# Threshold attention and Fourier mixing on one core: the last group's two closing products without the inner level, u's forms spread between products, the last fold placed by hand

## The chip, the cores and the metric

The kernel runs on one core of one Trainium2 chip. The time is the device time of one execution in microseconds (us), the median of several runs. Lower is better. Line numbers (L1306) are those of the kernel before the change, unless it is said otherwise.

## The reference, cut to what matters

```python
scores = scale * q @ k.T                       # 8 batches x 8 heads, 576 x 576, 64 deep
attn = softmax of the scores within tau of each row's maximum, 0 elsewhere
x = attn @ v, heads side by side               # (8, 576, 512)
u = x + real(fft(fft(x, axis=1), axis=2))
un = (u - mean(u)) / sqrt(var(u) + 1e-6)       # over the 512 channels
out = u + relu(un @ w_ch1) @ w_ch2             # w_ch1 512 x 2048, w_ch2 2048 x 512
```

All is computed in fp32.

## The kernel before, in words

**The two halves.** The attention half goes through 8 batches, 4 pairs of heads each, 5 tiles of queries a pair: 160 steps. A batch's weighted values are folded by symmetry (`fold_rows`, DVE L678 to L694 for the last pair of a batch; `fold_chunks` L709 and L710; further folds in `mixing`, L731 to L740) and turned by small matrix products into u, kept transposed in `u_t` (py L750, pa L767 and L771, u_t L792 and L796).

The channel half takes the 4608 rows of u in 9 groups of 512. Group 0 is computed plainly (`channels`). Groups 1 to 8 go through `two_level`. The first stage multiplies by w1: 4 parts with 7 products each (a Strassen scheme in Winograd's form, in the order 1, 2, 5, 6, 4, 7, 3), PE L1163. The second multiplies by w2 with two levels of the same scheme: 7 outer products (`L1` = 1, 2, 5, 4, 6, 7, 3), each made of 7 inner ones (`J`) of 4 matmuls, PE L1306, 28 matmuls to an outer product. Normalisation is applied at the end, where a product is added to u with the factor `rstd` (`Rows.add`, DVE L863); `Rows.store` (L870) writes 128 finished rows from SP's queue.

**The forms.** A Strassen scheme multiplies sums and differences of its blocks. On the side of u there are four per group: t1, t2, -t4, t3 (`u_form`, L1087; two instructions each, on DVE for groups 7 and 8, on POOL before). The inner forms of the left operand of the second stage are s1 and s2 on DVE and s3 and s4 on POOL (`l2_forms`, L1144), made during the outer product before; the outer ones are `l1_form` (L1121: a21, s1 and a12, a quarter at a time). The forms of the weights are made once, during groups 0 and 1, by `w1_forms` and `w2_forms` (L977), and written to DRAM as blocks of 128x512: 28 in f1 and 49 in f2, seven per outer product. A form of w2 is stored by `keep`: two inner blocks (L987), the last (L991), and the four computed ones (L998) out of a room in `w1[3]` which the next form's blocks are written into.

**What sets the order.** The code is written in the order in which each engine shall work; there is no scheduler behind it. `fill` lets as much of the channel half go ahead as the budget of a slot allows; in the steps of the attention half three calls of it stand between parts of the softmax. The weight blocks come in loads of four (`ensure`, L1036) into a ring of three buffers, two loads ahead. Small jobs of DVE and POOL in the second stage are placed by hand at slots (outer product, inner product) with `at_slots`. All PSUM tiles of the products come out of four banks.

**The first stage's evictions.** In a part, product 1 is copied from its bank by ACT (L1172), product 2 is added by DVE (L1100) and put through relu by ACT (L1105), product 5 is copied by ACT (L1174). Product 6 accumulates in product 1's bank and DVE adds it to product 5's copy (L1100). Product 4 is copied by ACT (L1182). Product 7 accumulates in that same first bank and is added to two results at once (L1100, 128x1024); product 3 follows in a bank of its own. In the code all four u forms are issued ahead of the first product.

**The second stage's results.** v_u, v_11, v_22, v_21 and v_12 hold outer results in seven inner pieces each (896 columns). ACT copies (L1321) or DVE adds (L1323, L1326) each outer product into them. `gather` sums the seven inner pieces of a result in five additions (L1213), and `finish` adds them to u (L863). For groups 1 to 7 the gathers are on POOL, in the next group's time. For the last group there is no next one: they are on DVE, in slots of the last product (3), whose bank is evicted in pieces.

**The end of the attention half.** The loop over steps runs three steps beyond the last (L1635), in which the last tile's weights, the last product with v (`values_in_parts`, pv L627, copied by ACT L634), the last fold and the last `mixing` come.

Of the kernel before, what the change touches and what calls it, by code (L numbers as in the profile page):

```python
# [9 lines left out]
FP32 = mybir.dt.float32  # L10
# [37 lines left out]
def kernel(  # L48
# [874 lines left out]
    J = (1, 2, 5, 4, 6, 7, 3)  # L923
    HH = HID // 2
    f1 = dram.tile([128, 28, 512], FP32, name="f1")
    f2 = dram.tile([128, 49, 512], FP32, name="f2")

    def w1_forms():

# [37 lines left out]
    def w2_forms():  # L967
# [11 lines left out]
        def keep(m, at):  # L979
            x = b[at]  # L980
            i = 7 * L1.index(m)
            to = f2[:, i : i + 7, :].rearrange("p j (s n) -> p j s n", n=128)
            quarter = {
                (k, n): x[:, 4 * k : 4 * k + 4, 128 * n : 128 * n + 128]
                for k in range(2) for n in range(2)
            }
            nc.sync.dma_start(  # L987
                out=f2[:, i : i + 2, :].rearrange("p j (s n) -> p (j s) n", n=128),
                in_=x[:, :, 0:128],
            )  # L990
            nc.sync.dma_start(out=to[:, 6], in_=quarter[1, 1])  # L991
            t1, minus_t4, t2, t3 = (room[:, j] for j in range(4))
            combine(nc.vector, t1, quarter[0, 1], quarter[0, 0])
            combine(nc.gpsimd, t3, quarter[1, 1], quarter[0, 1])
            yield
            combine(nc.vector, t2, quarter[1, 1], t1)
            combine(nc.gpsimd, minus_t4, quarter[1, 0], t2)
            nc.sync.dma_start(out=to[:, 2:6], in_=room)  # L998
            yield
# [25 lines left out]

    PER = 4
    LOADS = [(f1, 28, k) for k in range(0, 28, PER)] + [(f2, 49, k) for k in range(0, 49, PER)]
    issued = 0

    def ensure(n):  # L1030

        nonlocal issued
        while issued <= n and issued < (NG - 1) * len(LOADS):
            src, count, k = LOADS[issued % len(LOADS)]
            n_blocks = min(PER, count - k)
            nc.sync.dma_start(  # L1036
                out=w1[issued % 3][:, 0 : 512 * n_blocks].rearrange("p (j n) -> p j n", n=512),
                in_=src[:, k : k + n_blocks, :],
            )
            issued += 1  # L1040

    def block(g, second, index):

# [18 lines left out]
    def two_level(g, rows):  # L1062
# [25 lines left out]
                    out=out_[:, c], in0=in0[:, c], in1=in1[:, c], op=ALU.subtract  # L1088
                )

        u_form(t1, b[0, 1], b[0, 0])
        u_form(t2, b[1, 1], t1)
        u_form(minus_t4, b[1, 0], t2)
        u_form(t3, b[1, 1], b[0, 1])
        right = {
            1: b[0, 0], 2: b[1, 0], 3: b[1, 1], 4: minus_t4, 5: t1, 6: t2, 7: t3,
        }
# [50 lines left out]
        for part in range(4):  # L1148
# [4 lines left out]
            for at, m in enumerate(ORDER):  # L1153
# [30 lines left out]
                elif m == 7:  # L1184
                    twice = bass.AP(
                        tensor=bank.tensor, offset=bank.offset,
                        ap=[list(bank.ap[0]), [0, 2], [1, 512]],
                    )
                    add(both, twice)
                    relu(both)  # L1190
                else:
                    add(h01, bank[:, :])
                    relu(h01)
                next(forms, None)
                tick()
                if part == 3 and g > 1 and at in (2, 3, 5):
# [23 lines left out]
        def gather(eng, v):  # L1220
# [7 lines left out]
                plus(eng, v[:, 2:4], twice(v[:, 5])),  # L1228
            ]

        def finish(i, n, v):
            if wanted:
                wanted.pop().factors()
# [20 lines left out]
            for jn, job in zip(slots, jobs, strict=True):  # L1254
                side.setdefault((at, jn), []).append(job)

        for at in range(6):
            def next_form(at=at):
                if at not in coming:
                    coming[at] = l2_forms(L1[at + 1])  # L1260
# [9 lines left out]
        at_slots(4, (1, 2, 4, 6), l1_form(a12, a12, s1_tile, (P, P, P, P)))  # L1270
        at_slots(2, (0, 1, 2, 3, 4), gather(P, v_11))
        at_slots(4, (2, 4), [lambda n=n: finish(0, 0, v_11)[n]() for n in range(2)])
        at_slots(
            5, (0,), [lambda: P.tensor_tensor(out=v_12, in0=v_u, in1=v_22, op=ALU.add)]
        )
        if g < NG - 1:
            at_slots(6, (0, 1), [plus(P, v_22, v_u), plus(P, v_21, v_u)])
        else:
            at_slots(6, (0, 0), [plus(V, v_22, v_u), plus(P, v_21, v_u)])
            at_slots(6, (1, 1, 1, 1, 1), gather(V, v_22))  # L1280
            at_slots(6, (2, 2), finish(1, 1, v_22))
            at_slots(6, (2, 2, 3, 3, 3), gather(V, v_21))
            at_slots(6, (4, 4), finish(1, 0, v_21))
            at_slots(6, (4,), [stores(2, 3)])
            w = v_12.rearrange("p (j n) -> p j n", n=128)
            at_slots(6, (4,) * 4, [
                plus(V, w[:, 1:5:3], twice(w[:, 0])), plus(V, w[:, 6], w[:, 2]),
                plus(V, w[:, 6], w[:, 4]), lambda: rows.add(0, slice(256, 384), w[:, 1]),
            ])
            second = bass.AP(  # L1290
                tensor=w.tensor, offset=w[:, 3].offset, ap=[list(w.ap[0]), [-128, 2], [1, 128]]
            )
            at_slots(6, (5,) * 4, [
                plus(V, w[:, 5], w[:, 4]), plus(V, w[:, 2:4], twice(w[:, 5])),
                lambda: rows.add(1, slice(256, 512), second), stores(1),
            ])
        for at, m in enumerate(L1):
            for jn, j in enumerate(J):
                cut = g == NG - 1 and m == 3
                if jn in (0, 4) or cut and jn > 4:  # L1300
                    bank = ps.tile([128, 512], FP32, tag="mm", bufs=4, name="po")
                c0 = 0 if cut and jn > 4 else 128 * (jn % 4)
                to = bank[:, c0 : c0 + 128]
                right_ = block(g, True, 7 * at + jn)
                for s in range(4):
                    nc.tensor.matmul(  # L1306
                        to, lefts[m][j][:, s], right_[:, 128 * s : 128 * (s + 1)],
                        start=(jn in (0, 4) or cut and jn > 4) and s == 0, stop=s == 3,
                        skip_group_check=True,
                    )  # L1310
                if jn in (3, 6) or cut and jn > 3:
                    first, end = (0, 512) if jn == 3 else (512, NV)
                    if cut and jn > 3:
                        first, end = 128 * jn, 128 * jn + 128
                    src = bank[:, 0 : end - first]

                    def here(v):
# [3 lines left out]
                        nc.scalar.copy(here({1: v_u, 5: v_22, 4: v_21}[m]), src)  # L1321
                    elif m == 2:
                        V.tensor_tensor(out=here(v_11), in0=here(v_u), in1=src, op=ALU.add)  # L1323
                    else:
                        to = here(v_12 if m == 3 else v_u)
                        V.tensor_tensor(out=to, in0=to, in1=src, op=ALU.add)  # L1326
                while held:
                    held.pop(0)()
                held.extend(side.get((at, jn), ()))
                while held and not holding:  # L1330
                    held.pop(0)()
                if jn == 3 and at < 4:
                    rows.load((2, 3, 0, 1)[at])
                    if at == 3:
# [4 lines left out]
            background()  # L1339
            if m != 3:  # L1340
                yield 2048
        if g == NG - 1:
            w = v_12.rearrange("p (j n) -> p j n", n=128)
            rows.add(0, slice(384, 512), w[:, 6])
            rows.store(0)
            return
        for v in (v_22, v_21, v_12):
            pending.extend(gather(P, v))
# [283 lines left out]

    late.append(True)

    for i in range(2 * per_batch, total + 3):  # L1635


        n, t = divmod(i, NT)
# [52 lines left out]
            load_v(n + 1)  # L1691
        if t == 4 and n + 2 < B * NPAIR:
            load_pair(n + 2)
    ended.append(True)
    per_slot = cost(0) / 40
    while mixes or work:
# [47 lines left out]
```

## Time and profile before

| | |
|---|---|
| median of 3 runs (lowest, highest) | 1607.57 us (1606.21, 1608.24) |
| profiled execution, its own time | 1605.7 us |
| its span | 1603.8 us |
| granted TensorE clock, mean | 0.988 |
| PE busy | 1537.4 us, 96% |
| DVE, ACT, POOL busy | 69%, 57%, 51% |
| chain that ended last | PE 76%, DVE 14%, ACT 4%, issue 2%, POOL 2%, DMA 1% |
| last stage of groups 7 and 8 (first matmul) | 1400.5, 1498.7 us |

The profile is one execution on the chip. A row of the timeline gives the start in us from the span's start, the duration, the engine, the line, the operation, what it writes and reads with the shape, and how many instructions were merged; in brackets stands the idle time of the engine before it and what ended that. PE is the matmul, PEld the weight load beside it. An fp32 matmul of the code stands as two rows in the trace. Ends of matmuls are modelled. SPq is the queue of SP, which issues nearly all transfers.

### The profile page before, as it was taken

How to read it: one execution, taken by the hardware profiler on the slowest of the kernel's cores; microseconds unless marked ns; L12 is line 12 of the kernel's file. 1: busy time of each engine (PE TensorE's matmuls, PEld its weight loads, DVE VectorE, ACT ScalarE, POOL GpSimd, SP SyncE). 2: the span in 40 equal slices, each digit the busy share in tenths (PEclk: the TensorE clock that was granted, in tenths of full speed). 3: DMA queues.
4: the chain of work that ended last, by engine and by line, in shares of the span. 5: the costliest groups of instructions: out<-in, count | busy, mean ns of one | idle time of the engine just before them, and what ended most of it. 6: DMA issues, size and time to landing. Idle time of an engine off the chain costs nothing.

```text
span 1603.8 us, 27061 instructions
## 1 busy us (share of the span) xinstructions
PE 1537.4 (96%) x9770; PEld 1189.2 (74%) x9770; DVE 1105.6 (69%) x2165; ACT 908.4 (57%) x1873; POOL 811.7 (51%) x1014
## 2 busy tenths in 40 slices
PE   8999979999999999999999999999999999999997
PEld 4555445555787778877787878787887778879997
DVE  7997886845869566766577566856676656746547
ACT  5774665554655666656666666656665665223121
POOL 6784664034455552536254724455263625537646
PEclk9999999999999999999999999999999999999998
DMA  6423221555956264634564355626463534546655
GB/s 158 131 57 115 75 76 36 175 158 164 291 159 203 72 182 125 182 104 141 141 175 140 113 159 145 191 69 180 123 185 108 154 113 158 191 157 237 235 193 190
DMA packets 245499, 239.05 MB, mean 149 GB/s; under 512 B 196947, under 2 KB 214869, under 8 KB 225014
## 3 DMA queue, kind: packets, MB, share of 16 engines
q1 hardware_dynamic: 242854, 237.02, 49.1%
q8 instruction: 78, 1.28, 0.3%
q10 hardware_dynamic: 2512, 0.30, 0.2%
q14 instruction: 55, 0.45, 0.1%
HBM read 207.50 MB, written 29.62 MB: 148 GB/s over the span
## 4 chain that ended last, share of the span: by engine, by line
PE 76%; DVE 14%; ACT 4%; issue 2%; POOL 2%; DMA 1%; SPq 0%; DVEq 0%; ACTq 0%; POOLq 0%
PE ph L1163 24%; PE po L1306 17%; PE pv L627 8%; PE sc L427 7%; PE pw L596 6%; PE po L901 4%; PE ph L877 2%; PE py L750 2%; DVE e L467 2%; PE sc L433 1%; PE pa L767 1%; PE pe L578 1%; PE pa L771 1%; DVE neg L451 1%; ACT e L512 1%
## 5 line engine op out<-in xcount | busy, mean ns | idle before, releaser
L512 ACT ACTIVATE e<-sc,neg 128x576 f32<-128x576 f32 x216 | 158.6, 734 | 139.8 <-DVE neg L506 139.4
L506 DVE TENSOR_REDUCE neg<-sc 128x1 f32<-128x576 f32 x216 | 154.0, 749 | 112.0 <-PE sc L427 104.1
L1306 PE MATMUL po<-w,w_all 128*128 128x128 f32 x1792 | 229.1, 278 | 0.7 <-ACT ends L584 0.7
L1306 PEld LDWEIGHTS po<-w,w_all 128*128 128x128 f32 x1792 | 214.7, 193 | 10.2 <-issue 5.5
L1100 DVE TENSOR_TENSOR hs<-ph,hs 128x512 f32<-128x512 f32 (+1 forms) x128 | 105.1, 821 | 158.5 <-PE ph L1163 104.0
L1109 POOL TENSOR_TENSOR w<-hs 128x512 f32<-128x512 f32 x32 | 42.1, 1320 | 318.9 <-ACT hs L1105 245.1
L596 PE MATMUL pw<-ident,e 128*128 128x128 f32 x1152 | 172.1, 276 | 18.0 <-ACT x_first L634 9.1
L1163 PE MATMUL ph<-u_t,w 128*128 128x256 f32 x768 | 180.5, 381 | 0.5 <-DMA w<-f 0.4
L527 DVE SCALAR_TENSOR_TENSOR e<-sc,thr,e 128x576 f32<-128x576 f32 x216 | 168.1, 811 | 17.7 <-ACT thr L516 17.7
L427 PE MATMUL sc<-kT,qT 64*128 64x288 f32 x1024 | 170.3, 432 | 7.9 <-DVE e L467 7.9
L598 ACT COPY e_t<-pw 128x512 f32<-128x512 f32 x256 | 148.5, 594 | 45.8 <-PE pw L596 44.6
L540 ACT ACTIVATE e<-e,den 128x576 f32<-128x576 f32 x216 | 157.6, 775 | 16.6 <-DVE den L534 15.4
L596 PEld LDWEIGHTS pw<-ident,e 128*128 128x128 f32 x1152 | 136.3, 142 | 36.3 <-ACT x_first L634 10.1
L1163 PE MATMUL ph<-w_all,w 128*128 128x256 f32 x672 | 157.0, 382 | 2.9 <-DVE hs L1100 1.8
L1163 PEld LDWEIGHTS ph<-u_t,w 128*128 128x128 f32 x768 | 141.2, 190 | 23.4 <-issue 4.4
L1105 ACT ACTIVATE hs<-hs 128x512 f32<-128x512 f32 (+1 forms) x96 | 74.1, 772 | 122.0 <-DVE hs L1100 120.8
L1163 PEld LDWEIGHTS ph<-w_all,w 128*128 128x128 f32 x672 | 123.5, 190 | 25.6 <-issue 6.2
L427 PEld LDWEIGHTS sc<-kT,qT 64*128 64x128 f32 x1024 | 93.9, 186 | 62.9 <-issue 32.8
L1213 POOL TENSOR_TENSOR w_all<-w_all 128x128 f32<-128x128 f32 (+2 forms) x160 | 118.5, 758 | 29.9 <-DVE w_all L1326 22.4
L1306 PE MATMUL po<-w,hs 128*128 128x128 f32 x960 | 126.3, 279 | 0.0
L1306 PEld LDWEIGHTS po<-w,hs 128*128 128x128 f32 x960 | 116.2, 193 | 9.4 <-issue 7.2
L792 POOL TENSOR_TENSOR u_t<-x,tmp 128x289 f32<-128x289 f32 (+1 forms) x45 | 34.5, 766 | 104.8 <-DVE tmp L787 104.8
(221 smaller groups left out, 2985.1 us busy)
## 6 DMA issues: line engine op xcount, KB each, us to landing
w<-f SPq DMA_DIRECT2D x152, 1024.0 KB, 4.9
hs<-in_moe_w_ch_dram SPq DMA_DIRECT2D x23, 512.0 KB, 4.6
q_in<-in_q_dram SPq DMA_DIRECT2D x128, 72.0 KB, 3.9
out_dram<-u SPq DMA_DIRECT2D x36, 256.0 KB, 2.5
k_in<-in_k_dram SPq DMA_DIRECT2D x124, 72.0 KB, 3.0
v_in<-in_v_dram SPq DMA_DIRECT2D x64, 128.0 KB, 4.7
f<-w SPq DMA_DIRECT2D x14, 512.0 KB, 4.0
f<-w SPq DMA_DIRECT2D x7, 1024.0 KB, 4.4
```

The costliest lines, as they stand in the source:

```text
L427: nc.tensor.matmul(sc[j][:, c, 0:HALF], qT[hp, 128 * t : 128 * t + 128], kT[hp, k0 + HALF * c : k0 + HALF * (c + 1)], start=True, stop=True,)
L506: nc.vector.tensor_reduce(out=neg[:, j : j + 1], in_=sc[j][:, :, 0:HALF], axis=AXIS_XY, op=ALU.max, negate=True,)
L512: nc.scalar.activation(out=ej, in_=sc[j][:, :, 0:HALF], func=ACT.Exp, bias=neg[:, j : j + 1], scale=1.0)
L527: nc.vector.scalar_tensor_tensor(out=ej, in0=sc[j][:, :, 0:HALF], scalar=thr[:, j : j + 1], in1=ej, op0=ALU.is_ge, op1=ALU.mult, accum_out ...
L540: nc.scalar.activation(out=e[:, S * j : S * (j + 1)], in_=e[:, S * j : S * (j + 1)], func=ACT.Copy, scale=den[:, j : j + 1],)
L596: nc.tensor.transpose(pw[:, c, :], e[:, c0 : c0 + 128], ident[:, :])
L598: nc.scalar.copy(e_t[:, 4 * j : 4 * j + 4, qs], pw[:, :, :])
L627: nc.tensor.matmul(pv[64 * j : 64 * j + 64, 0:m], vt[:, 2 * c + j, :], e_t[:, 4 * j + c, 0:m] if c < 4 else ends[:, 0, 0:m], start=(c == 0 ...
L1100: nc.vector.tensor_tensor(out=to, in0=bank, in1=to if other is None else other, op=ALU.add)
L1163: nc.tensor.matmul(bank[:, 256 * q : 256 * q + 256].rearrange("p (two n) -> p two n", two=2), left[:, 256 * c + 128 * q : 256 * c + 128 * ...
L1213: return lambda: eng.tensor_tensor(out=to, in0=to, in1=other, op=ALU.add)
L1306: nc.tensor.matmul(to, lefts[m][j][:, s], right_[:, 128 * s : 128 * (s + 1)], start=(jn in (0, 4) or cut and jn > 4) and s == 0, stop=s == ...
```

## The change

1. **Products 7 and 3 of the last group** have no inner scheme any more. Each is done as 4 blocks of 8 matmuls into two banks (one for each 128 rows), straight from the left operand and the four quarters of w2's outer form. For this `keep` writes seven more blocks of 128x512 to f2 (four at form 3, three at form 7), and the last group's loads end with one of three and one of four blocks. Product 6 is added to v_22 and v_21 at once (DVE), v_u is added to v_22 on POOL and to v_21 on DVE earlier, both results are gathered together (five additions of double width on DVE) while product 7 runs, and go to all four tiles of rows. Products 7 and 3 are added to u directly from PSUM. v_12 isn't formed in this group.
2. **The u forms of groups 7 and 8**: only t1 stands ahead of the first product; t2, -t4 and t3 follow behind the evictions of products 2, 5 and 6 of the first part.
3. **The end of the attention half** is written out in place of the loop's three extra steps. PE's order stays the same. On ACT, the copy of the last pv (L634) moves behind a copy of an outer product and four copies of u. On DVE, `fold_chunks` (L709, L710) comes ahead of one inner form, an eviction and two adds to u, and another inner form comes ahead of two fold instructions.

```diff
-    f2 = dram.tile([128, 49, 512], FP32, name="f2")
+    f2 = dram.tile([128, 56, 512], FP32, name="f2")
...
             nc.sync.dma_start(out=to[:, 6], in_=quarter[1, 1])
+            for n, at_ in {7: ((49, (1, 0)), (50, (1, 1)), (51, (0, 1))),
+                           3: ((52, (0, 0)), (53, (1, 0)), (54, (1, 1)), (55, (0, 1)))}.get(m, ()):
+                nc.sync.dma_start(
+                    out=f2[:, n].rearrange("p (s n) -> p s n", n=128), in_=quarter[at_]
+                )
...
+    ALL_LOADS = LOADS * (NG - 2) + LOADS[:16] + [(f2, 52, 49), (f2, 56, 52)]
...
-        u_form(t1, b[0, 1], b[0, 0])
-        u_form(t2, b[1, 1], t1)
-        u_form(minus_t4, b[1, 0], t2)
-        u_form(t3, b[1, 1], b[0, 1])
+        u_forms = [
+            (t1, b[0, 1], b[0, 0]), (t2, b[1, 1], t1), (minus_t4, b[1, 0], t2),
+            (t3, b[1, 1], b[0, 1]),
+        ]
+        while len(u_forms) > (3 if g >= NG - 2 else 0):
+            u_form(*u_forms.pop(0))
...
+                if at > 0 and u_forms:
+                    u_form(*u_forms.pop(0))
                 next(forms, None)
                 tick()
...
+            at_slots(3, (1,), [plus(P, v_22, v_u)])
+            at_slots(4, (0,), [plus(V, v_21, v_u)])
+            at_slots(5, (0, 0, 1, 1, 2), gather_both())
+            at_slots(5, (2, 3), finish(0, 1, v_22))
+            at_slots(5, (3, 3), finish(1, 1, v_22))
+            at_slots(6, (0, 0), finish(1, 0, v_21))
+            for n in range(2):
+                at_slots(
+                    6, (1,), [lambda n=n: rows.add(2 + n, slice(0, 512), twice(plain[7][n]))]
+                )
+                at_slots(6, (1,), [stores(2 + n)])
...
+        def plain_product(at, m):
+
+            x = a[m].rearrange("p (k s i n) -> p k i s n", k=2, i=2, n=128)
+            banks = plain[m] = [
+                ps.tile([128, 512], FP32, tag="mm", bufs=4, name="po")[:, 0:256] for _ in range(2)
+            ]
+            for jn, (n, k, at_) in enumerate(((0, 0, 0), (0, 1, 1), (1, 1, 2), (1, 0, 3))):
+                right_ = plain_block(m, at_)
+                for i in range(2):
+                    for s in range(4):
+                        nc.tensor.matmul(
+                            banks[i][:, 128 * n : 128 * n + 128], x[:, k, i][:, s],
+                            right_[:, 128 * s : 128 * (s + 1)],
+                            start=jn == 0 and s == 0, stop=jn % 2 == 1 and s == 3,
+                            skip_group_check=True,
+                        )
+                slot(at, jn)
...
+        if whole:
+            while held:
+                held.pop(0)()
+            for n in range(2):
+                rows.add(n, slice(256, 512), plain[3][n])
+                rows.store(n)
             return
...
-    for i in range(2 * per_batch, total + 3):
+    for i in range(2 * per_batch, total):
...
+    values = values_in_parts(B * NPAIR - 1, 1)
+    next(values, None)
+    fill(True)
+    while held:
+        held.pop(0)()
+    next(values, None)
+    while folds:
+        fold_more()
+    last_fold = fold_rows(B * NPAIR - 1)
...
+    start_batch(B - 1)
+    for _ in range(3):
+        mix(1)
+        fill(True)
```

## The prediction

> **What bounds the kernel now.** I read the page first, then the chain of waits from 1380 us on, then the timelines of PE, DVE and SP where the change touches them.
>
> ```profile
> span 1603.8 us, 27061 instructions
> ...
> PE 1537.4 (96%) x9770; PEld 1189.2 (74%) x9770; DVE 1105.6 (69%) x2165; ACT 908.4 (57%) x1873; POOL 811.7 (51%) x1014
> ```
>
> PE is busy 96% of the span, so time is to be had only where PE idles (66 us in all) or after its last matmul. The change touches three such places. The end, from the timeline:
>
> ```profile
> 1588.57 4.71 DVE L1213 TENSOR_TENSOR w_all<-w_all 128x896 f32<-128x896 f32 x6
> ...
> 1589.99 2.84 PE L1306 MATMUL po<-w,w_all 128*128 128x128 f32 x24
> ...
> 1599.32 0.48 DVE L863 SCALAR_TENSOR_TENSOR u<-w_all,rstd,u 128x256 f32<-128x256 f32 x1
> ...
> 1600.04 0.35 DVE L863 SCALAR_TENSOR_TENSOR u<-w_all,rstd,u 128x128 f32<-128x128 f32 x1
> ```
>
> PE's last row ends at 1592.83; DVE works on to 1600.39, and the last store ends the span 3.4 us later. So 7.56 us of gathers and adds lie behind PE. Second, the start of group 7 (start, duration, engine, line; in brackets the idle time before it and what ended it):
>
> ```profile
> 1405.84 1.77 DVE L1087 TENSOR_TENSOR w_all<-u_t,t_room 128x256 f32<-128x256 f32 x2 [1.98 <-POOL u_t L792]
> ...
> 1406.89 4.06 PE L1163 MATMUL ph<-w_all,w 128*128 128x256 f32 x16 [0.96 <-DVE w_all L1087]
> 1407.53 1.27 DVE L1087 TENSOR_TENSOR w_all<-u_t,w_all 128x256 f32<-128x256 f32 x2
> ...
> 1408.72 1.54 DVE L1087 TENSOR_TENSOR w_all<-u_t 128x256 f32<-128x256 f32 x2
> ...
> 1410.18 0.68 DVE L1100 TENSOR_TENSOR hs<-ph,hs 128x512 f32<-128x512 f32 x1
> ...
> 1412.03 0.69 DVE L1100 TENSOR_TENSOR hs<-ph,hs 128x512 f32<-128x512 f32 x1 [1.17 <-ACT hs L1174]
> ...
> 1412.78 1.99 PE L1163 MATMUL ph<-w_all,w 128*128 128x256 f32 x8 [1.83 <-DVE hs L1100]
> ```
>
> All four u forms (L1087) stand on DVE ahead of the first eviction (L1100, 1410.18); ACT's copy of product 5 waits behind that eviction's relu, the second eviction waits for the copy, and product 7, which adds into that bank, waits until 1412.78. Third, the last fold:
>
> ```profile
> 1384.18 0.80 PE L750 MATMUL py<-dim_c,f 128*128 128x128 f32 x2 [2.91 <-DVE f L731]
> 1384.77 1.92 PE L1306 MATMUL po<-w,w_all 128*128 128x128 f32 x8
> ```
>
> PE waits 2.91 us, and the eight rows behind that take 1.92 where eight take 1.06 elsewhere, the next eight 1.91: with the granted clock at 0.91 over 1360 to 1400, the wait costs about 1.7 us more than itself.
>
> **Products 7 and 3 plain: PE.** The old product is 28 matmuls, 56 rows in the trace (each stands twice), and takes 6.25 us (chain of waits, "PE po L1306 x56"), 0.1117 us a row. The plain one is 32 matmuls, 64 rows, 7.15 us; the operand shapes are the same, so I take the same price. Two of them: +1.79 us, all on the path, because PE has no gap from 1498.68 on. PE's end moves from 1592.83 to 1594.62. Their weights are loads of 768 KB and 1 MB, asked for at the first and the fifth block of product 6 (1573.9 and 1577.5); with the 4.9 us of w<-f they land by 1582.4, while the blocks are wanted at about 1582.0 (first, landing 1578.8) and 1587.3: at nothing. The cover is about 3 us; a landing of 9.1 us, the longest in this trace, would cost about 1 us.
>
> **The same: DVE and POOL.** Removed behind PE: the inner forms of products 7 and 3 (L1144), v_12, and the gathers of three results. What is left, in DVE's new order: product 6's second add (768 elements from PSUM; between the rows of 512 at 0.69 and 1024 at 1.22, so 0.96) starts when product 6 ends, 1580.36, and ends at 1581.3. Five joint gathers, two of 512 elements at 0.69 and three of 256 at 0.41 (the quickest L1087), 2.6 us, to 1583.9. Six adds of 128x256 at 0.44 (the pair at 1593.19 took 0.88), to 1586.6. Plain product 7 ends at 1587.5; its two adds of 128x512 take 0.75 each (L863 u<-po), to 1589.0, followed by the stores of rows 2 and 3 on SP, which has no load left behind them. Then DVE is free, 5 us before PE ends. Product 3's first bank is complete eight rows before the end, so its add runs beside PE; the second starts at 1594.65 and takes 0.48 (0.75 for 512 less 0.27 for 256 elements), to 1595.13, against 1600.39 before: **-5.3 us**. The last stores follow close together before and after, 3.4 us.
>
> Here a rule speaks against the change. Rows: DVE's L1144 of 128x512 took 0.69 us at best and 1.58 us in the mean of the four from w that stood beside POOL work. The Trainium skill, page "SBUF — State Buffer", section "Who interferes with whom", says that a DVE instruction with two SBUF inputs is shut out while a GpSimd instruction that reads SBUF holds the shared ports. The new gathers are of this kind, and POOL now does v_22's sum (2.1 us) and all of a12's four parts (1.27 to 1.75 each). Laid out from 1569.5, these and product 6's forms (1.65 and 1.27, the latter not before 1573.3) end at about 1581, as the gathers start. By the free price the sum is 1589.0, as above; by the rule, were POOL busy throughout, two gathers at 1.58, three at 0.94 and six adds at 1.31 make 13.8 us in place of 5.2, and DVE ends product 7's adds at about 1596.6 (0.94 from the slowest L1087, 1.31 from the pair of L863 at 1374.02). I take the free price, since POOL's list is over; the adds from PSUM have one SBUF tensor and stay out of it.
>
> **The u forms.** New order in groups 7 and 8: t1, first eviction, t2, -t4, second eviction, t3. In group 7, t2 still waits for u_t until 1405.84 (POOL, not moved), so the 0.96 us before product 6 stays. The first eviction now runs at 1404.2, in DVE's idle time. Product 6 ends at about 1409.0, product 4 at 1410.7; the second eviction runs 1409.1 to 1409.8, t3's halves come at 1410.5 and 1411.1; product 7 starts at about 1410.7 instead of 1412.78: **-2.1 us**. PE then shows no idle up to group 8, so the gain is kept to the end. In group 8, which has no such wait today, an eviction of 0.69 now stands ahead of t2: with T the end of product 2, t2's halves come at T+1.4 and T+2.1 to 2.3, and PE wants them at T+1.7 and T+2.2: +0.1 (0 to 0.5). Together **-2.0**. Bounds: nothing (each wait returns at t3), and -2.8 (both idle times of group 7).
>
> **The last v product and fold.** PE's order is unchanged there. ACT's copy of x (L634) moves behind five evictions, from 1361.53 to about 1364.8, done at 1365.2; the fold's first step waits for DVE's statistics until 1365.76 anyway. On DVE two fold steps (0.78 and 0.79) move ahead of four other instructions, and one form moves earlier; DVE works without a gap from 1365.76 to 1386, with the same rows ahead of L731, so PE's wait of 2.91 stays. POOL's s4 for product 7 comes about 1.3 us later, to 1376.3, and is wanted at 1378.0. Cost 0; bounds -4.6 (the whole wait and the slow rows behind it) and +0.5 (POOL's overlap falls worse).
>
> **Seven more stores of blocks (f<-w_all, 256 KB).** They stand on SP's queue in the stage of 358 to 417 us: four behind 358.17, three behind 406.83. Queued behind them: v's loads, the row swap at 369.63, the store of the forms' room (L998), and the weight loads. Engine times by stretch (last two numbers: DMA share and GB/s), then SP's timeline:
>
> ```profile
> 400.00:420.00 20.00, 19.23 (x109) 14.95 (x108) 19.52 (x32) 12.06 (x23) 14.11 (x16) 1.00 0.90 291
> ```
>
> ```profile
> 406.83 0.58 SPq L991 DMA_DIRECT2D f<-w_all  x1
> 412.40 0.33 SPq L998 DMA_DIRECT2D f<-w  x1
> ```
>
> Issue is 0.58 each, 1.7 to 2.3 us in a row, and SP stands free for 2.2 and 5.0 us before L998 (v's loads end at 363.61, L991 at 407.41). The DMA engines are 90% busy, so three stores of 0.79 MB at 291 GB/s push the queue out by 2.7 us. L998 then lands at 412.4 + 4.4 + 2.7 = 419.5; its room is wanted by POOL at 419.20 and DVE at 420.00. I take **+0.3**. Below nothing isn't possible, as nothing is removed. By the page's price (same page, "The DMA setup-cost knee": about 2 us plus bytes at 436 GB/s) a store is an estimated 2.6 us, three one after another 7.8, and the room comes free at 421.6: 1.6 us late. By the landing row, 4.6 us, see the last rival.
>
> **Sum.** -5.3 - 2.0 + 0 + 0.3 = -7.0 us. Against the profiled execution's own time of 1605.7 (span 1603.8 and 1.9 around it) this is 1598.7; the median of the runs is 1607.57, 1.87 above it, so I predict 1600.6.
>
> **Rivals.**
> 1. The forms give nothing: DVE is late again at t3, with POOL's gathers (8.75 us from 1406.42) beside it. For: L1087 rows range from 0.41 to 0.95. Against: t3 needs 1.5 us and has 1.6. 1607.57 - 5.0 = 1602.6.
> 2. DVE isn't clear when PE ends, by the port rule above: its last add ends near 1597.6 rather than 1595.13, so the tail gives 2.8. Against: POOL's list ends at 1581. 1607.57 - 2.8 - 2.0 + 0.3 = 1603.1.
> 3. The fold's move frees PE's wait and the slow rows, 4.6 us. For: two steps stand earlier. Against: DVE has no gap ahead of L731. 1600.6 - 4.6 = 1596.0.
> 4. Slower: the new stores drain one at a time at 4.6 us (the landing of f<-w_all). Product 7's three end at 425.2, L998 lands at 429.6, and DVE's t1 at 420.00 waits 9.6 us, with softmax and evictions of an in-order DVE queued behind it (35.65 us busy of 40 here, so some 8 reach PE); product 3's four end at 381.2, L998 at 385.6, t1 at 376.71 waits 8.9, of which 4.4 are DVE's own idle time. Together +12.5: 1607.57 - 7.3 + 12.5 = 1612.8. It decides the sign once these waits pass 7.3 us. Against: loads and stores overlap in this trace at 291 to 298 GB/s.
>
> **How the numbers follow.** Likeliest case 0.66 (1599 to 1602), rivals 0.13, 0.08, 0.08 and 0.05. The range 1597.0 to 1604.2 takes in half of the third rival, all but the worse part of the second, and leaves out the last. A measurement here tells 0.2%, 3.2 us, from no change, so the border is 1604.4: faster 0.87, same 0.08 (the second rival's worse half, forms and tail both short), slower 0.05.
>
> **What would show it.** Right: PE's last two products at 7.15 us each without idle, DVE ending about 0.5 us behind PE, product 7 of group 7 starting 2 us sooner behind product 1, PE's wait for L731 still near 2.9. Wrong: idle PE ahead of product 3, L863 in a row of several behind PE, new waits of DVE or POOL L977 for DMA near 376 or 420, or a fold wait that is gone.

## The result, and the profile after

| | before | after |
|---|---|---|
| median (lowest, highest), 9 runs each on one chip | 1607.57 us (1604.78, 1610.17) | 1600.40 us (1598.40, 1604.87) |
| ratio, 95% interval | | 0.9962 (0.9953 to 0.9972): 6.1 us faster (4.5 to 7.6) |
| profiled execution, own time | 1605.7 us | 1599.3 us |
| its span | 1603.8 us | 1596.8 us |

The predicted time was 1600.6 us. The recorded ratio is not that of the two medians, which lie 7.2 us apart; the 6.1 us are the ratio times the median before. In the new kernel L1344 is the plain product, L1365 the inner products, L1382 and L1385 DVE's additions of outer products, L1259 the joint gather, L1100 the u forms, L1115 the first stage's additions, L1178 its matmuls, L994 the new stores, L1003 the store of the forms' room.

The page of the kernel after, the span and its first part:

```profile
span 1596.8 us, 27063 instructions
...
PE 1538.9 (96%) x9786; PEld 1191.1 (75%) x9786; DVE 1097.3 (69%) x2148; ACT 908.5 (57%) x1873; POOL 805.1 (50%) x1009
```

PE has 16 rows and 1.5 us of work more, DVE 8.3 us less, and the span is 7.0 us shorter: PE's work was not what went. The end of the kernel after, from the timeline:

```profile
1575.07 6.17 POOL L1136 TENSOR_TENSOR hs<-hs,w 128x512 f32<-128x512 f32 x4
...
1578.76 14.46 PE L1344 MATMUL po<-w,hs 128*128 128x128 f32 x128
1580.04 0.94 DVE L1382 TENSOR_TENSOR w_all<-w_all,po 128x768 f32<-128x768 f32 x1
1581.01 2.64 DVE L1259 TENSOR_TENSOR w_all<-w_all 128x512 f32<-128x512 f32 x5
1583.57 2.45 DVE L863 SCALAR_TENSOR_TENSOR u<-w_all,rstd,u 128x256 f32<-128x256 f32 x6
1585.94 1.40 DVE L863 SCALAR_TENSOR_TENSOR u<-po,rstd,u 128x512 f32<-128x512 f32 x2
...
1592.36 0.48 DVE L863 SCALAR_TENSOR_TENSOR u<-po,rstd,u 128x256 f32<-128x256 f32 x1 [5.02 <-PE po L1344]
1593.25 0.48 DVE L863 SCALAR_TENSOR_TENSOR u<-po,rstd,u 128x256 f32<-128x256 f32 x1 [0.41 <-PE po L1344]
```

Both plain products stand as one row of 128 without a gap. POOL's list ends at 1581.24, as the gathers begin at 1581.01. DVE is done with product 7 at 1587.34, waits 5.0 us for product 3, and ends at 1593.73, 0.51 us behind PE (1593.22). Before, it was 7.56 us behind.

The start of group 7 after, from the timeline (the last row is cut by the edge of the view):

```profile
1404.71 0.69 DVE L1115 TENSOR_TENSOR hs<-ph,hs 128x512 f32<-128x512 f32 x1 [0.45 <-PE ph L1178]
...
1406.24 1.77 DVE L1100 TENSOR_TENSOR w_all<-u_t,t_room 128x256 f32<-128x256 f32 x2 [0.84 <-POOL u_t L792]
...
1407.30 6.08 PE L1178 MATMUL ph<-w_all,w 128*128 128x256 f32 x24 [0.97 <-DVE w_all L1100]
1407.94 1.27 DVE L1100 TENSOR_TENSOR w_all<-u_t,w_all 128x256 f32<-128x256 f32 x2
...
1409.74 0.69 DVE L1115 TENSOR_TENSOR hs<-ph,hs 128x512 f32<-128x512 f32 x1 [0.53 <-PE ph L1178]
1410.34 1.42 DVE L1100 TENSOR_TENSOR w_all<-u_t 128x256 f32<-128x256 f32 x2
...
1413.22 2.97 PE L1178 MATMUL ph<-u_t,w 128*128 128x256 f32 x13
```

The first eviction now comes before the last three forms (1404.71, against 1410.18), and the idle 1.83 us ahead of product 7 is gone. The wait for u_t stays (0.97). Not all is won, though: the 24 rows of products 6, 4 and 7 take 6.08 us here and 5.34 in group 8, so some 0.7 us of small stops is hidden in the row. The view of PE's weight loads shows 0.27 and 0.30 of it, each behind one half of t3 (L1100).

The last fold after, from the timeline:

```profile
1384.59 0.80 PE L750 MATMUL py<-dim_c,f 128*128 128x128 f32 x2 [2.82 <-DVE f L731]
...
1385.18 1.92 PE L1365 MATMUL po<-w,w_all 128*128 128x128 f32 x8
```

PE waits as long as before, and the slow rows follow as before. The stores, SP's timeline after, and then the engines' busy times in the stretch around them (the last three numbers are clock, DMA share and GB/s):

```profile
408.05 4.54 SPq L994 DMA_DIRECT2D f<-w_all  x3
413.06 0.33 SPq L1003 DMA_DIRECT2D f<-w  x1
```

```profile
400.00:420.00 20.00, 19.22 (x109) 14.88 (x108) 18.55 (x30) 12.61 (x24) 13.86 (x15) 1.00 0.97 313
```

Three stores hold SP for 4.5 us, 1.5 each, where one took 0.58 before; the stretch moves 313 GB/s in place of 291, and PE's busy time is the same to 0.01 us. The room of the forms comes free later (waits of the kernel after from 340 to 440 us: in total, times, longest):

```profile
POOL w L977 <- DMA f<-w: 13.3, 3, 5.4
...
DVE w L977 <- DMA f<-w: 3.7, 2, 2.7
```

In the kernel before:

```profile
POOL w L977 <- DMA f<-w: 6.6, 2, 4.2
...
DVE w L977 <- DMA f<-w: 2.7, 1, 2.7
```

POOL waits twice as long, and no new wait of PE comes of it: in their own stage the seven stores are hidden.

**Where the time went.** The same landmarks in both traces:

| stretch | before | after | difference |
|---|---|---|---|
| from the span's start to a store of u at 342 us | 341.95 | 342.50 | +0.55 |
| 342 to 433, store of u to the store of the last form's room | 91.05 | 91.29 | +0.24 |
| from there to the last product with v | 925.57 | 925.29 | -0.28 |
| to group 7's first matmul | 41.91 | 41.80 | -0.11 |
| to group 8's first matmul | 98.20 | 96.45 | -1.75 |
| to PE's last row | 94.15 | 95.89 | +1.74 |
| from there to DVE's last instruction | 7.56 | 0.51 | -7.05 |
| from there to the span's end | 3.41 | 3.07 | -0.34 |

The rows add up to -7.0. The change touches nothing that runs in the first stretch, which is between 341.1 and 344.8 us long in the 13 profiled executions.

### The profile page after: what moved, and what is told of

The parts are those of the page before. It is cut to its first block, busy times and chain, and to the rows that moved or that the text cites. A ratio compares the mean times of both kernels' runs of the same rounds, so it can differ in the third digit from the quotient of the medians.

```text
span 1596.8 us, 27063 instructions
## 1 busy us (share of the span) xinstructions
PE 1538.9 (96%) x9786; PEld 1191.1 (75%) x9786; DVE 1097.3 (69%) x2148; ACT 908.5 (57%) x1873; POOL 805.1 (50%) x1009
## 4 chain that ended last, share of the span: by engine, by line
PE 77%; DVE 14%; ACT 4%; issue 2%; POOL 2%; DMA 2%; SPq 0%; DVEq 0%; ACTq 0%; POOLq 0%
PE ph L1178 24%; PE po L1365 17%; PE pv L627 8%; PE sc L427 7%; PE pw L596 6%; PE po L901 4%; PE ph L877 2%; DVE e L467 2%; PE py L750 2%; PE sc L433 1%; PE pa L767 1%; DVE neg L451 1%; PE pe L578 1%; PE pa L771 1%; PE po L1344 1%
## 5 line engine op out<-in xcount | busy, mean ns | idle before, releaser
L1365 PE MATMUL po<-w,w_all 128*128 128x128 f32 x1728 | 220.9, 278 | 0.8 <-ACT ends L584 0.8
L1365 PEld LDWEIGHTS po<-w,w_all 128*128 128x128 f32 x1728 | 206.9, 193 | 10.2 <-issue 5.5
L1115 DVE TENSOR_TENSOR hs<-ph,hs 128x512 f32<-128x512 f32 (+1 forms) x128 | 105.2, 822 | 157.8 <-PE ph L1178 101.7
L1178 PE MATMUL ph<-u_t,w 128*128 128x256 f32 x768 | 180.5, 381 | 0.7 <-DMA w<-f 0.4
L596 PEld LDWEIGHTS pw<-ident,e 128*128 128x128 f32 x1152 | 136.7, 142 | 36.3 <-ACT x_first L634 10.1
L1178 PEld LDWEIGHTS ph<-u_t,w 128*128 128x128 f32 x768 | 141.2, 190 | 23.5 <-issue 4.4
L1178 PE MATMUL ph<-w_all,w 128*128 128x256 f32 x672 | 157.1, 382 | 1.1 <-DVE w_all L1100 1.0
L1178 PEld LDWEIGHTS ph<-w_all,w 128*128 128x128 f32 x672 | 123.4, 190 | 23.9 <-issue 4.9
L1365 PE MATMUL po<-w,hs 128*128 128x128 f32 x912 | 120.2, 279 | 0.0
L1365 PEld LDWEIGHTS po<-w,hs 128*128 128x128 f32 x912 | 110.5, 193 | 9.4 <-issue 7.2
```

The lines of the kernel that those rows point to most:

```text
L596: nc.tensor.transpose(pw[:, c, :], e[:, c0 : c0 + 128], ident[:, :])
L1115: nc.vector.tensor_tensor(out=to, in0=bank, in1=to if other is None else other, op=ALU.add)
L1178: nc.tensor.matmul(bank[:, 256 * q : 256 * q + 256].rearrange("p (two n) -> p two n", two=2), left[:, 256 * c + 128 * q : 256 * c + 128 * ...
L1365: nc.tensor.matmul(to, lefts[m][j][:, s], right_[:, 128 * s : 128 * (s + 1)], start=jn in (0, 4) and s == 0, stop=s == 3, skip_group_check ...
```

## The experiments

Theory at this point: the change is three separate parts, -5 from the tail, -2 from the forms, nothing from the last fold, and stores that are hidden. Rivals: that the gain of the tail is due to the new order at the fold, that the forms' gain is lost again downstream, and that the stores cost more than their stage shows. A change in us is the recorded ratio, which has a 95% interval, times the median of the kernel before on the same chip; it can differ by 1 us from the difference of the two medians.

### Each part alone

Plain products and stores alone: the kernel after, with

```diff
-        while len(u_forms) > (3 if g >= NG - 2 else 0):
+        while u_forms:
...
-    for i in range(2 * per_batch, total):
+    for i in range(2 * per_batch, total + 3):
```

and without the written-out end.

> Only the plain products of the last group, with their seven stores; u forms and the end of the attention half as before. My theory (three separate gains: tail 5.3 us, forms 1.8 us as the profile after shows, end of the attention half nothing, stores a cost of a few tenths): 1607.6 - 5.3 + 0.3 = 1602.6, and DVE ends 0.5 us behind PE. If instead the tail was shortened by the earlier start of group 7, so that the parts need each other: above 1604.

Measured: 1603.1 against 1606.3 us, ratio 0.9976 (0.9969 to 0.9983), -3.9 us. That is 1.1 us less than expected; the interval (2.7 to 5.0) just reaches 5.0. In its trace DVE ends 0.51 us behind PE (1594.48, 1593.97), as in the whole change:

```profile
1593.11 0.48 DVE L863 SCALAR_TENSOR_TENSOR u<-po,rstd,u 128x256 f32<-128x256 f32 x1 [5.03 <-PE po L1344]
1594.00 0.48 DVE L863 SCALAR_TENSOR_TENSOR u<-po,rstd,u 128x256 f32<-128x256 f32 x1 [0.41 <-PE po L1344]
```

The forms alone: the kernel before, with the list of the diff and `if at > 0 and u_forms: u_form(*u_forms.pop(0))` behind the evictions.

> Only the u forms of groups 7 and 8 spread between the products. Theory: product 3 of group 7's first part starts 1.8 us sooner behind product 1, group 8 loses nothing, 1607.6 - 1.8 = 1605.8. Rival (the wait comes back later, at the tail, which is DVE's): PE ends sooner, but DVE ends as late as before, 1607.6.

Measured: 1604.26 against 1606.3, ratio 0.9987 (0.9981 to 0.9994), -2.1 us. DVE still ends 7.60 us behind PE, and the first stage's row is that of the whole change (timeline of this kernel, its matmuls at L1165):

```profile
1406.06 6.09 PE L1165 MATMUL ph<-w_all,w 128*128 128x256 f32 x24 [0.97 <-DVE w_all L1087]
```

The end of the attention half alone: the kernel before with the three extra steps written out as in the diff.

> Only the end of the attention half written out as in the change. Theory: no change, 1607.6 within 0.7, and PE's wait for the fold (DVE L731) stays between 2.7 and 3.0 us. Rival: the fold's move is worth the wait and the slow rows behind it, 4.6 us, 1603.0.

Measured: 1605.82 against 1606.3, ratio 0.9998 (0.9990 to 1.0006), -0.3 us: nothing that can be told from zero. PE waits for L731 as before (timeline of PE):

```profile
1386.46 0.79 PE L750 MATMUL py<-dim_c,f 128*128 128x128 f32 x2 [2.83 <-DVE f L731]
```

The three add up to -3.9 - 2.1 - 0.3 = -6.3, against -6.1 for the whole. Within intervals of about 1 us each, the parts don't help or hinder each other.

### The stores

Seven stores alone, with nothing that reads them; the kernel before with the added lines of `keep`:

```diff
+            for n, at_ in {7: ((49, (1, 0)), (50, (1, 1)), (51, (0, 1))),
+                           3: ((52, (0, 0)), (53, (1, 0)), (54, (1, 1)), (55, (0, 1)))}.get(m, ()):
+                for more in (0,):
+                    nc.sync.dma_start(
+                        out=f2[:, n + more].rearrange("p (s n) -> p s n", n=128), in_=quarter[at_]
+                    )
```

> The kernel before with the seven new stores once each, which nothing reads. The plain products alone gave 1.1 us less than my terms (3.9 against 5.0); if the stores cost more than the 0.3 us that I gave them, it is seen here: 1.0 to 1.6 us slower. If they are hidden, as I predicted: 0 to 0.5 us slower, and the 1.1 us is the spread between runs.

Measured: 1608.83 against 1605.62, ratio 1.0021 (1.0012 to 1.0031), +3.4 us, while its own stage grew by 0.4 us only (91.48). So it was run again, with more runs:

> The kernel before plus the seven stores once more, as in the earlier run of it, which was 3.4 us slower than before by its median while the stretch of its own stores (342 to 433 us) grew by only 0.4 us. If the stores cost what that stretch shows, the profiled execution shows 91.0 to 91.5 us there and about 925.6 us from 433 us to the first product with v, and the median is before's plus 0.2 to 1 us. If the stores slow the attention that follows, the second stretch shows about 928 us again and the median is again 3 us over before's.

Measured: 1607.55 against 1606.06, ratio 1.0011 (1.0005 to 1.0018), +1.8 us (0.8 to 2.9). Its own stage took 91.41 us, and the attention behind it 928.09, against 925.57 before. Neither expectation was met as a whole; what the second stretch holds is told under the clock, below.

Each store three times (`more in (0, 7, 14)`), 21 in all:

> The kernel before with the seven new stores of the change, each made three times to different places (21 stores, 5.5 MB), which nothing reads. Theory (a store costs nothing until the forms' room is freed later than the next form wants it; seven just fit): the room's store lands some 8 us later than before at both places, DVE and POOL wait there, and of that 3 to 8 us reach PE: 1611 to 1616. Rival (the queue's stores are hidden whatever their number, since PE's work here doesn't depend on the forms for long): within 1 us of 1607.6.

Measured: 1615.89 against 1606.3, ratio 1.0063 (1.0051 to 1.0076), +10.1 us. From three views of its trace, which is that of the slowest of its six runs (1619.71) (SP's timeline, PE's timeline, the waits of 340 to 440 us):

```profile
361.95 12.92 SPq L995 DMA_DIRECT2D f<-w_all  x12
```

```profile
419.97 3.02 PE L427 MATMUL sc<-kT,qT 64*128 64x288 f32 x8 [6.49 <-DVE e L527]
```

```profile
POOL half L678 <- DMA x<-swap: 21.4, 2, 18.6
DVE w L977 <- DMA f<-w: 17.3, 5, 8.1
```

Twelve stores hold SP's queue for 12.9 us; the row swap queued behind them comes late, POOL waits up to 18.6 us for it (10.0 in the kernel after), DVE up to 8.1 for the room of the forms, and PE 6.5 for DVE. The slower rival had the kind of chain right, a late room that holds DVE and with it PE, but not the places: it had 8.9 us of DVE at 376.71 and 9.6 at 420.00, each behind its own stores. Here DVE waits 3.1 us at the first place, and the wait of 8.1 ends at 418.49, for a room stored at 411.56, ahead of the other nine stores (from 416.52 on). So it is the twelve that reach PE. With 7 stores PE's busy time is whole; with 21 the stretch from 342 us on grew by 11.9 us.

### Is DVE clear because POOL is idle?

The kernel after, with eight additions on POOL beside the gathers, into columns that nothing reads any more:

```diff
             at_slots(5, (0, 0, 1, 1, 2), gather_both())
+            spare = quadrant(1, 1)
+            at_slots(5, (0,) * 8, [
+                lambda n=n: P.tensor_tensor(
+                    out=spare[:, 512 * (n % 4) : 512 * (n % 4) + 512],
+                    in0=spare[:, 512 * (n % 4) : 512 * (n % 4) + 512],
+                    in1=a12[:, 512 * (n % 4) : 512 * (n % 4) + 512], op=ALU.add,
+                ) for n in range(8)
+            ])
```

> The changed kernel with eight POOL additions of 128x512 in SBUF put beside the joint gathers of the last group, into columns that nothing reads later. By the port rule: the five gathers take about 6 instead of 2.64 us and the six adds about 7.9 instead of 2.45, product 7's adds end near 1592 to 1595, while the adds from PSUM keep their 0.7 us; the end moves by 0 to 1 us. Rival (DVE doesn't mind POOL here): both rows as in the change, no difference at the end.

Measured: 1602.76 against 1606.19, ratio 0.9977 (0.9967 to 0.9987), 2.4 us over the kernel after (1.4 over its second set of runs, below). The timeline of its end:

```profile
1579.68 6.69 DVE L1259 TENSOR_TENSOR w_all<-w_all 128x512 f32<-128x512 f32 x5
1579.88 11.84 POOL L1320 TENSOR_TENSOR hs<-hs 128x512 f32<-128x512 f32 x8
1586.29 6.51 DVE L863 SCALAR_TENSOR_TENSOR u<-w_all,rstd,u 128x256 f32<-128x256 f32 x6
1592.72 2.18 DVE L863 SCALAR_TENSOR_TENSOR u<-po,rstd,u 128x512 f32<-128x512 f32 x4
```

The same eleven DVE instructions take 13.2 us in place of 5.1, and DVE ends 3.0 us behind PE (1594.90, 1591.90) in place of 0.5; at most 1 us more had been expected. Shape hardly matters while POOL works. By the single records, the four gathers that ran wholly beside POOL took 1.37 to 1.75 us (three of 256 elements, one of 512; 0.42 to 0.68 in the kernel after) and four of the six additions 1.48 to 1.49; the last two additions came behind POOL and took 0.47. The four additions from PSUM come behind POOL's last row and show nothing of this, but they begin late. The prediction's second rival priced DVE's delay at 2.5 us (1597.6 less 1595.13); it is 2.5 (3.0 less 0.5). It didn't come about in the kernel after because POOL had finished, as its timeline shows.

### Product 7 with its inner level again

The plain form costs PE 0.9 us a product. Product 7 doesn't end the kernel, so it could keep the inner level: the kernel after with `if whole and at > 5` in place of `at > 4`, the loads and stores to match (four new stores, not seven), and product 7 copied into v_12 by ACT, gathered by DVE and added to rows 2 and 3 beside product 3.

> The changed kernel with product 7 of the last group done by the inner scheme again (28 matmuls, four inner forms, ACT copies it, DVE gathers it alone and adds it to two tiles twice), product 3 plain. Theory (only the last product needs to be plain, as DVE has 5 us to spare beside it): PE does 0.9 us less, DVE's extra gathers and adds of about 4 us fit beside product 3, 1599.5. Rival (DVE is not clear when PE ends, for it has two more inner forms beside product 6): 1 us or more of adds behind PE, 1601 or more.

Measured: 1600.29 against 1606.19, ratio 0.9957 (0.9943 to 0.9971), no difference from the kernel after that could be told. The timeline of its end, DVE alone:

```profile
1585.91 1.60 DVE L1226 TENSOR_TENSOR w_all<-w_all 128x256 f32<-128x256 f32 x5
1587.44 1.67 DVE L863 SCALAR_TENSOR_TENSOR u<-w_all,rstd,u 128x256 f32<-128x256 f32 x4
...
1589.02 0.87 DVE L863 SCALAR_TENSOR_TENSOR u<-po,rstd,u 128x256 f32<-128x256 f32 x2
```

PE is 0.9 us shorter, but the gather and four more additions put DVE 0.93 us behind PE in place of 0.51: from the end of product 6 the tail is 0.5 us shorter. Another 0.5 us lies outside the span: an execution takes 1.9 us more than its span in all five runs here, and 2.3 to 2.5 in all 15 of the kernel after. Together that is 1 us, too little for these runs to tell, so product 7 plain is a tie or a small loss. The tail is won by the rest: product 3 plain, and the gathers of v_22 and v_21 moved beside product 7. No run separates these two, that is, keeps product 3's inner level behind the early gathers.

### The fold ahead of the inner forms

The remaining wait of PE is for L731. In the kernel after DVE's two rows of L731 stand behind two inner forms, and beside POOL's (timeline of the kernel after):

```profile
1382.50 1.71 POOL L1159 TENSOR_TENSOR w_all<-hs 128x512 f32<-128x512 f32 x1
1383.01 2.99 DVE L731 SCALAR_TENSOR_TENSOR f<-f,factors 128x304 f32<-128x304 f32 x2
```

The kernel after with more of the mixing issued ahead of the products' own work:

```diff
-    for _ in range(3):
-        mix(1)
+    for early in (1, 2, 0):
+        mix(early)
         fill(True)
```

> The changed kernel, and the last three fold instructions (DVE L731 twice, L740) moved ahead of an eviction and two inner forms, nothing else. Theory (PE's wait of 2.8 us is set by DVE's order alone): the folds are done near 1381.5, the wait goes, PE waits up to 0.7 us for an inner form of product 3 instead, and the rows behind it run at their usual pace: -2.8 - 1.7 + 0.7 = -3.8, 1596.6. Rival (the inner forms are just as urgent, so that the wait only changes its name): 1600.4.

Measured: 1598.33 against 1606.19, ratio 0.9947 (0.9935 to 0.9960), -8.5 us. Its timeline:

```profile
1380.23 0.97 DVE L731 SCALAR_TENSOR_TENSOR f<-f,factors 128x304 f32<-128x304 f32 x2
...
1382.11 0.94 PE L750 MATMUL py<-dim_c,f 128*128 128x65 f32 x6
...
1382.88 1.06 PE L1365 MATMUL po<-w,w_all 128*128 128x128 f32 x8
```

L731 is out of POOL's way (0.97 us for the pair, not 2.99), PE doesn't wait for it, and the eight rows behind take 1.06. A wait of 0.97 us for an eviction (L1385, at 1385.80) is new. The stretch from the last product with v to group 7 took 37.47 us in place of 41.80: 4.3 us in this trace.

Both together, this and product 7 with its inner level:

> The changed kernel with both later edits: the last fold instructions ahead, and product 7 of the last group by the inner scheme. If they add up, by the segments of their traces (4.3 us from product 7 of group 6 to the first product of group 7; 0.5 us from product 6 to the last add): 4.8 us below the changed kernel, about 10.9 us below the kernel before, ratio 0.9932. If the fold's gain is given back later: 6.6 us below it.

Measured: 1596.25 against 1605.62, ratio 0.9944 (0.9932 to 0.9956), -9.0 us. The kernel after, beside it on the same chip:

> The changed kernel itself, beside the others of this call, for a comparison on one chip: 6.1 us below the kernel before.

Measured: 1600.80 against 1605.62, ratio 0.9968 (0.9956 to 0.9980), -5.1 us. So this version is faster than both kernels, than the kernel after by 3.9 us (9.0 less 5.1; the medians are 4.6 apart), where 4.8 were expected. Product 7 made no difference by itself that could be told, so the fold is left as the cause of most of it.

### The clock, and where the stores' extra microseconds are

Two results lie well off what was expected: the stores alone cost 3.4 us, and the fold gave 2.4 where 3.8 were expected. Both have to do with rows of PE at double length, which come in some executions and not in others. The trace's record of the granted clock shows stretches at half clock. In each of the 13 profiled executions they lie on one grid of 3.41 us, and its offset from the span's start differs from execution to execution (1.25 us after, 0.09 in the kernel with product 7 inner). Busy times by stretch, laid on that grid, around the last fold (the second number is PE's busy time, the third last the clock); the kernel after:

```profile
1380.24:1383.65 3.41, 1.53 (x15) 1.39 (x13) 3.38 (x3) 0.00 (x0) 3.41 (x2) 1.00 0.37 84
1383.65:1387.06 3.41, 2.47 (x11) 2.47 (x12) 3.41 (x5) 0.63 (x2) 2.01 (x2) 0.50 0.53 223
1387.06:1390.48 3.42, 3.42 (x18) 3.42 (x17) 1.07 (x2) 0.63 (x1) 2.89 (x2) 0.50 0.01 2
1390.48:1393.89 3.41, 3.41 (x31) 2.96 (x29) 0.29 (x1) 0.62 (x2) 1.23 (x1) 1.00 0.31 58
```

and the kernel with product 7 inner, which has the same code and the same wait of 2.82 us there:

```profile
1379.08:1382.49 3.41, 1.63 (x16) 1.49 (x14) 3.38 (x3) 0.00 (x0) 3.41 (x2) 1.00 0.33 72
1382.49:1385.90 3.41, 2.27 (x18) 2.08 (x18) 3.41 (x5) 0.63 (x2) 2.12 (x2) 1.00 0.56 235
```

In the first, most of the idle time lies in one window so that PE is busy for 45% of it, and the next two windows run at half clock; in the second it is 48%, and the clock stays. At this fold all windows at 38% to 46% (7 executions) were followed by half clock, and that at 48% was not; in three more executions the wait is split so that PE is busy for over half of each window, and the clock stays. The price: from the last product with v to group 7 it is 41.8 to 41.95 us with the half clock, in every trace that has it, and 39.5 without, so 2.3 us. Elsewhere the busy share by itself doesn't decide: in the kernel before, a window with PE busy for 61% of it (from 103.25 us) was followed by half clock, and one with 46% (from 1410.56) was not. What else counts is open.

The attention stretch from 433 us to the last product with v has such windows at the ends of batches, and their number goes with its length:

| windows at half clock | executions | us |
|---|---|---|
| 4 | before, after twice, and five others | 924.9 to 925.7 |
| 5 | additions on POOL | 926.7 |
| 6 | stores once, twice; stores threefold; fold with product 7 inner | 927.6 to 928.1 |

So the 2.5 us that both traces with the stores alone show behind their own stage are two more windows at half clock, 1.3 us each. The kernel after has the same stores and four windows, in both its traces. Over all runs of the first set with the stores alone the mean granted clock has a median of 0.984, against 0.987 for the kernel before beside it: the missing 0.003 of 1604 us is 9.6 us at half clock, 2.8 windows, some 3.7 us by the price of a window here. That estimate is the upper one: over the 100 executions of the kernel before in these sets, a straight line of time against clock gives 0.6 us for 0.001, so 1.8 us for 0.003. The clock covers between half and all of the 3.4. In the second set both medians are 0.986, so there it explains the trace, which is one execution, but not the 1.8 us of all runs. What these are stays open.

For the fold moved ahead, the same reading gives the range: its stretch takes 37.5 us, against 41.8 with and 39.5 without the half clock, so 4.3 us are gained in some executions and 2.0 in others. All runs put it 2.4 us ahead of the kernel after in its first set (8.5 less 6.1) and 3.4 in its second (8.5 less 5.1), each against the kernel before on its chip.

## Why the prediction was right, point by point

**The tail** (-5.3): right in its terms. From group 8's first matmul to DVE's end the trace has 96.40 in place of 101.71 us, -5.31. PE's end moved by +1.74 (predicted +1.79), DVE is 0.51 us behind it (0.5). It was right to take the free price and not the rule's: POOL's list was over at 1581.2 (predicted 1581). The rule itself, in the page "SBUF — State Buffer", section "Who interferes with whom", holds when POOL is busy: the experiment has 2.5 us for it, as priced. The plain products and their stores alone gave 3.9 us by their runs where these terms make 5.0; the difference is within the interval.

**The u forms** (-2.0): right in kind, -1.75 in the trace, -2.1 by the runs of the forms alone. Group 7's product 3 starts 12.34 us behind the group's first matmul in place of 14.13, so 1.8 there and not 2.1: the halves of t3 took 1.42 us for the pair where 1.3 was allowed, and PE stops shortly for each. Group 8, priced at +0.1, shows no new stop.

**The fold** (0): right, -0.3 by the part alone, which its interval doesn't tell from zero, and -0.1 in the trace. That the slow rows cost 1.7 us on top of the wait was true of the profiled execution and is not of every execution. The third rival's price of 4.6 was nearly right for another edit: 4.3 in that trace once L731 did move.

**The stores** (+0.3): right for their stage (+0.24), by another way than argued. Their issue was priced at 0.58 us each and took 1.4 to 1.5; SP had free time to hold most of it. By the runs of the stores alone they cost 3.4 us in one set, of which the clock covers between half and all, and 1.8 (0.8 to 2.9) in the other, which it doesn't cover. So the term may be too small by 1 or 2 us, and where those would lie is open.

**The sum** (-7.0). The span became 7.0 us shorter, as summed; what the terms don't name (+0.55, -0.28 and -0.34 in the table) cancels. But the execution's own time fell by 6.4 only: 1599.3, where 1598.7 was predicted, since 2.5 us lie around the span after and 1.9 did before. This is no spread: it is 2.2 to 2.5 us in every run with both products plain and nothing added, and 1.7 to 2.0 in every run of the kernel before, of the other two parts, of the stores alone and of product 7 with its inner level. So the change costs some 0.5 us there, for which the prediction has no term; why is open. And the median lies 1.1 us above the profiled execution after, 1.87 before, by the spread between executions. The two nearly cancel, so the predicted 1600.6 is nearer to 1600.4 than its terms deserve. The recorded ratio gives -6.1 (4.5 to 7.6), and the sum lies within.

**The rivals.** That the forms give nothing is out (-2.1 alone). DVE held up by POOL is real at its price and didn't occur. The fold's gain was there to be had, by an order that the change didn't make. The slower case was right that stores ahead of the rest of the queue can reach PE, and wrong about the amount and the price: they held SP for 1.1 to 1.5 us each and didn't drain one at a time at 4.6, and three or four in a row don't reach PE, while twelve do.

## What to carry to other kernels

At the end of a kernel, count what stands behind PE's last matmul. The inner scheme saved 0.9 us of PE a product, but 7.6 us of DVE's gathers and additions stood behind the last one. For a product that isn't last, the plain form gained nothing here. How much of the 7 us is owed to the plain form and how much to gathering the other results earlier, these runs don't tell. In front of an in-order engine, put what frees a bank ahead of what is needed later. And when two traces differ by 1 to 3 us far from the change, look at the clock by stretch before giving the difference a cause.

## What the runs showed of the hardware that was not expected

An idle time of PE under one clock window was enough to halve the clock: 2.82 us of waiting in a window of 3.41, with PE busy for 45% of it, cost two windows at half clock and 2.3 us, and the same wait, 0.1 us of busy time more in its window, cost nothing. The Trainium skill, page "TensorE: Matmul & The Clock Gate", section "Part 1: The HAM clock gate", has the free-running window of 3413 ns and the two clocks, and the grid here agrees with it (3.41 us, 0.50 and 1.00); its table asks for an idle window of about 3.4 us, though, and these traces show that one partly busy will do, as a later passage of the same part says, without a figure, of frequent short idle times. A window at half clock was followed by another where PE was busy for 72% of it, and not where it was fully busy.

DVE's rows of two SBUF operands don't grow in proportion beside a busy POOL: next to POOL's of 1.48 us each they took 1.4 to 1.5 us whatever their size (one 1.75), about as long as one of POOL's, so the short ones suffer most: an addition of 128x256 went from 0.48 us to 1.49.
